# A linear-attention and maxout kernel that runs from a written table: another table, buffer lists cut to their users, and the gate copies taken out

## Chip, core and metric

One core of one Trainium2 chip. The metric is the device time of one execution, in microseconds; of three executions of the kernel before, the median is 287.12.

## What is computed

Two parts, one behind the other. Attention with a feature map, per batch `b` and head `h` (8 by 8, 576 tokens, 64 columns), and then a maxout layer over the 4608 tokens with all heads side by side (512 columns, 768 hidden):

```python
def phi(x):                       # w_phi: 64 x 128
    proj = x @ w_phi
    proj = proj - max(abs(proj), axis=-1)
    return concat(exp(proj), exp(-proj))
kv  = phi(k).T @ v                # 256 x 64 per head
num = phi(q) @ kv
den = phi(q) @ sum(phi(k), over tokens) + 1e-6
x   = (num / den), heads side by side      # 4608 x 512
h   = maximum(maximum(x @ w1, x @ w2), x @ w3)
out = h @ w_out
```

Inputs and output are float32; the matmuls run in bfloat16.

## The kernel before

The attention is cut into 16 units of four heads (`u` = 0 to 15; two units make a batch). The names below are those of the steps, as `Node` has them in its first argument:

- `L`, `L0`, `Lv`: loads of q, k and v. Unit 0 loads q and k in two halves each, in float32, through SP, and casts them (`C`, on DVE or ACT). Units 1 to 3 load q and k through POOL with a cast on the way, straight into `qk_bf`. From unit 4 on the loads are float32 and POOL casts. v is always loaded in float32 (`v_raw`), through SP or, in early units, POOL.
- `T`, `Tc`: the transposes. For units 0 to 3 PE transposes into PSUM and DVE copies to `qkT`; later units use the DMA transpose from SP (line 508).
- `G`: projections by `w_phi`, into `psq` and `psk`; `r`: DVE's absolute maxima (line 554) into `mqp` and `mk`; `ek`: ACT's exponentials of k (line 548).
- For q: in units 0 and 1 the maximum is subtracted by small products (lines 616 and 619); from unit 2 on PE turns the maxima (`R`), a copy makes `mT`, a small DMA (`V`, line 570, from SP or ACT) stores them as a row of `qkT`, and `M` (line 614) projects with them. `eq` is ACT's exponential of `M`.
- `E`, `va`, `vd`: ACT's correction factors `em`, POOL's multiplication of v by them (line 589).
- `K`, `kv`, `N`, `x`, `X`: the sums over tokens, their copy, the numerators with the denominator as a column, the division, and the transpose of the result into `xT` (PE in units 0 and 1, the DMA transpose at line 691 later).

The maxout layer is cut into nine chunks of 512 tokens (eight batches' first 512, and the rest of all). It uses differences of weights (`wd`, POOL or DVE, line 785): `up`/`up2` are the products by w2-w1 and w3-w1 (line 714), with the maxima on DVE and ACT, and `down` sums the straight product of x by w1 w_out (line 742) and the hidden part by w_out (line 747). w1 w_out is made on the chip (`wt`, `we`, `wm`, `mo`). `W` are the weight loads on POOL, in number four.

No loop sets the order. `PLAN` is a written table with one word for each of the 1473 steps: `163T4@18.3` is step 163 on PE (T; D is DVE, A is ACT, G is POOL, S is SP), the first buffer of its list that has no slot yet gets slot 4, and 18.3 us is the moment for which the table laid it out. `plan` reads the words in order and gives each step its engine and slots; the steps are then emitted in that order, so that each engine's queue is fixed. The moment is not enforced on the chip: an engine takes its next step as soon as what the step needs is there and its buffers are free. It is used once more, in `fill`, which puts idle products (line 842, a 128x512 matmul of ones into a PSUM bank that is free) into gaps of PE's queue that are over 0.35 us in the table (over 0.5 from 28 us on), one each 0.43 us up to 4.6 us and one each 0.26 us later.

The list `bufs` of a step says which buffers it uses; in this kernel it is read only by `plan`, to hand out the slots in the word, and by `fill`, for PSUM. A tile is made at its first use when the steps are emitted.

Three gates hold loads back. For u = 1, 2 and 3 a DVE copy of one element from `qkT` of unit u - 1 into `v_raw` of unit u is placed ahead of that unit's v load, which has to wait for it:

```python
gates.append(nd("gate", {"DVE": 0.1}, lambda src=src, col=col, raw=raw: nc.vector.tensor_copy(
    raw()[0:1, 0, 0:1], src()[0:1, col:col + 1]), [], [src, raw]))
```

Of the kernel before, what the change touches and what calls it, by code (L numbers as in the profile page):

```python
# [105 lines left out]
138A@23.2 103D@23.4 139T3@23.7 49A@23.7 105A@23.8 160G@23.9 130T4@23.9 162D@24.0 141A@24.3 127T5@24.3 140A@24.5  # L106
228D3@24.7 108D@24.8 131A@24.8 69T007@24.9 229S@24.9 119A1@25.3 111A@25.6 120G1@25.7 137A@26.0 133T3@26.3 71D@26.4
129A@26.5 113D@26.7 121G@26.8 182T006200@26.8 70A@27.0 74T70@27.1 134A@27.2 185D@27.3 1095T0@27.4 123A@27.7 186D@27.9
135A@28.0 124G@28.1 132A@28.5 75D0@28.5 76T6@28.7 184A@29.0 78T3@29.1 125G@29.2 72T4@29.4 1096A@29.4 79D1@29.6
1093T7@29.7 126A@29.9 110A@30.0 77D0@30.2 122G@30.3 1077G@30.5 183A@30.5 73D1@30.8 128A@31.0 177T03@31.1 1081G@31.2  # L110
172T16@31.3 179A@31.5 142T124@31.6 175D@31.7 174A@32.0 181D@32.3 1094A@32.5 176D@32.9 1079G@33.3 167T51@33.4 180D@33.5
144A@33.6 187T7@33.7 178A@33.8 80T4@34.0 190D@34.1 82T0@34.3 168A@34.3 81D@34.5 1097T3@34.5 83A@34.8 170D@34.8
143A@35.3 363G0@35.4 191D@35.4 171D@35.8 151T41@35.8 1098A@36.0 147T0@36.2 152D0@36.4 149T5@36.5 189A@36.5 364G@36.5
192T2@36.8 173A@36.8 145T3@36.8 148D1@37.0 1091T4@37.2 169A@37.3 150D0@37.6 1080G@37.6 188A@37.7 193D0@38.2 146D1@38.4
194S@38.5 230T6@38.5 1092A@38.7 232T0@39.1 195A0@39.1 231D0@39.3 365S1@39.3 234T1@39.6 197G0@39.7 155T7@39.8 233D@39.9
# [758 lines left out]
```

## Time and profile before

| | |
|---|---|
| three executions | 286.9, 287.12 and 290.07 us, median 287.12 |
| profiled execution, first to last instruction | 285.3 us (its own device time is not listed; the median lies 1.8 us above this span) |
| PE busy | 274.8 us, 96% |
| DVE, ACT, POOL busy | 208.4, 192.5, 125.0 us |
| idle products | 28, 9.51 us busy |
| mean granted clock of PE | 0.992 |
| DMA | 51.46 MB, 180 GB/s on average |
| last matmul's end to the end of the span | 3.4 us |

PE is nearly always busy. Matmuls are pipelined, so a busy PE is not PE at its peak, and the idle products are in its busy time as well. In rows of the timeline, `start, length, engine line op out<-in xcount [idle before <-releaser]`; PEld is PE's weight load, SPq and ACTq are issues of DMAs.

### The profile page before, as it was taken

The numbers are of one execution on the slowest core, as the hardware profiler recorded it, in microseconds if no ns is written. First come the engines' busy times: TensorE is split into PE (matmuls) and PEld (weight loads), VectorE is DVE, ScalarE is ACT, GpSimd is POOL, SyncE is SP. The second block draws the span as 40 slices with busy tenths as digits, with TensorE's granted clock in tenths as the row PEclk, the third lists the DMA queues.
The fourth block names the chain that finished last, engine by engine and source line by source line (L and its number), as shares of the span: only waits on it lengthen the run. The fifth ranks groups of instructions, "written<-read, shape, count | busy, mean of one in ns | idle before, by whom it ended". The sixth has DMA issues, their size and how long they took to land.

```text
span 285.3 us, 8441 instructions
## 1 busy us (share of the span) xinstructions
PE 274.8 (96%) x3485; PEld 155.7 (55%) x3522; DVE 208.4 (73%) x442; ACT 192.5 (67%) x445; POOL 125.0 (44%) x107
## 2 busy tenths in 40 slices
PE   8889999999999999999999999999999999999995
PEld 3557674565565555456565565555544664444442
DVE  2897899988999868688678779987975472227431
ACT  3798979997999987878868887779775400041001
POOL 9338999945923574417534950160080501000000
PEclk9997999999999999999999999999999999999999
DMA  7999979999899998988897998294420134153135
GB/s 192 203 284 262 312 144 305 341 239 250 221 293 196 225 232 280 251 156 202 258 251 272 268 199 182 99 182 81 82 62 3 27 54 90 37 110 76 37 85 173
DMA packets 67760, 51.46 MB, mean 180 GB/s; under 512 B 48778, under 2 KB 53002, under 8 KB 67722
## 3 DMA queue, kind: packets, MB, share of 16 engines
q1 hardware_dynamic: 62734, 43.38, 60.6%
q0 software_dynamic: 4576, 7.28, 12.1%
q8 instruction: 27, 0.44, 0.6%
q10 hardware_dynamic: 412, 0.28, 0.3%
q14 instruction: 11, 0.09, 0.1%
HBM read 34.67 MB, written 9.44 MB: 155 GB/s over the span
## 4 chain that ended last, share of the span: by engine, by line
PE 81%; DMA 8%; ACT 6%; POOL 1%; DVE 1%; issue 1%; ACTq 0%; POOLq 0%
PE ups L714 29%; PE ops L747 15%; PE ops L742 10%; PE psn L661 6%; PE kvps L643 6%; DMA qk_bf<-in_q_dram 5%; PE psm L614 5%; PE psq L535 4%; DMA qkT<-mT 3%; ACT Eq L627 3%; PE pm L811 2%; ACT Ek L548 2%; PE tps L493 1%; PE psq L530 1%; POOL qk_bf L458 1%
## 5 line engine op out<-in xcount | busy, mean ns | idle before, releaser
L714 PE MATMUL ups<-xT,w_bf 128*128 128x512 bf16 x415 | 101.5, 379 | 1.4 <-ACT Ek L548 0.5
L627 ACT ACTIVATE Eq<-psm 128x512 bf16<-128x512 f32 (+1 forms) x160 | 81.9, 582 | 15.6 <-PE psm L614 12.8
L589 POOL TENSOR_TENSOR vab<-v_raw,em 128x1152 bf16<-128x1152 f32 (+1 forms) x36 | 68.1, 1907 | 36.8 <-ACT em L585 27.9
L548 ACT ACTIVATE Ek<-psk 128x512 bf16<-128x512 f32 x128 | 73.5, 622 | 8.5 <-PE psk L535 5.8
L714 PEld LDWEIGHTS <-w_bf 128*128 128x128 bf16 x432 | 40.6, 98 | 45.4 <-issue 1.0
L720 DVE TENSOR_TENSOR hT<-hT,ups 128x512 bf16<-128x512 bf16 x54 | 36.4, 683 | 24.6 <-ACT hT L722 13.6
L554 DVE TENSOR_REDUCE mqp<-psq 128x4 bf16<-128x512 f32 (+1 forms) x80 | 49.0, 633 | 5.1 <-PE psk L535 2.9
L747 PE MATMUL ops<-wout_bf,hT 128*128 128x512 bf16 (+2 forms) x215 | 51.5, 373 | 0.5 <-issue 0.2
L554 DVE TENSOR_REDUCE mk<-psk 128x4 f32<-128x512 f32 x64 | 43.0, 683 | 0.7 <-PE psk L535 0.5
L747 PEld LDWEIGHTS <-hT 128*128 128x128 bf16 x222 | 21.1, 98 | 23.1
L668 DVE TENSOR_TENSOR x_sb<-psn,rden 128x320 bf16<-128x320 f32 x64 | 31.5, 492 | 2.2
L722 ACT ACTIVATE hT<-ups 128x512 bf16<-128x512 f32 x31 | 18.5, 615 | 21.1 <-PE ups L714 21.0
L755 ACT COPY osb<-ops 128x512 f32<-128x512 f32 (+2 forms) x17 | 9.6, 581 | 30.2 <-PE ops L747 12.7
L661 PEld LDWEIGHTS <-Eq 128*128 128x128 bf16 x640 | 24.9, 97 | 8.0
L755 DVE COPY osb<-ops 128x512 f32<-128x512 f32 x20 | 13.6, 689 | 20.1 <-PE ops L747 18.5
L661 PE MATMUL psn<-kv_sb,Eq 128*128 128x65 bf16 x640 | 26.8, 194 | 0.1
L742 PE MATMUL ops<-xT 128*128 128x512 bf16 x88 | 24.2, 379 | 0.4
L614 PE MATMUL psm<-qkT,wphi_m 128*128 128x512 bf16 (+1 forms) x70 | 22.3, 359 | 0.7 <-DMA qkT<-mT 0.6
L535 PE MATMUL psq<-w,qkT 64*128 64x128 bf16 x256 | 21.5, 217 | 0.5 <-DVE qkT L496 0.2
L476 POOL CAST qk_bf<-q_raw 128x1152 bf16<-128x1152 f32 x12 | 13.8, 1148 | 18.1 <-DMA q_raw<-in_q_dram 9.7
L535 PE MATMUL psk<-w,qkT 64*128 64x128 bf16 x256 | 21.3, 217 | 0.4 <-DVE mqp L554 0.4
L535 PEld LDWEIGHTS <-qkT 64*128 64x128 bf16 x512 | 14.8, 94 | 10.7 <-issue 8.1
(76 smaller groups left out, 272.6 us busy)
## 6 DMA issues: line engine op xcount, KB each, us to landing
out_dram<-osb SPq DMA_DIRECT2D x64, 128.0 KB, 2.5
v_raw<-in_v_dram SPq DMA_DIRECT2D x14, 576.0 KB
k_raw<-in_k_dram SPq DMA_DIRECT2D x11, 576.0 KB, 4.9
q_raw<-in_q_dram SPq DMA_DIRECT2D x11, 576.0 KB, 4.9
w_bf<-in_moe_w_dram POOLq DMA_DIRECT2D x3, 768.0 KB, 11.1
v_raw<-in_v_dram POOLq DMA_DIRECT2D x2, 576.0 KB, 13.7
qk_bf<-in_k_dram POOLq DMA_DIRECT2D x3, 288.0 KB, 13.4
qk_bf<-in_q_dram POOLq DMA_DIRECT2D x3, 288.0 KB, 13.6
```

Of the source, the lines that this page charges most:

```text
L535: nc.tensor.matmul(ps()[:, i, :], lhsT=cols[r, :], rhs=w2[r, c, :], start=True, stop=True)
L548: nc.scalar.activation(Ek[s]()[:, tiles_of(t0, n), :], of(1), EXP, scale=1.0 - 2.0 * s)
L554: nc.vector.tensor_reduce((mq, mk)[c]()[:, tiles_of(t0, n)], of(c), AXX, ALU.max, apply_absolute_value=True)
L589: (nc.vector if n_.eng == "DVE" else nc.gpsimd).tensor_tensor(vab()[:, g, t0:t1, 0:D], vb()[:, t0:t1, :], em()[:, g, t0:t1].unsqueeze(2).t ...
L614: nc.tensor.matmul(psm()[:, 0:w], lhsT=wphi_m, rhs=rhs, start=True, stop=True)
L627: nc.scalar.activation(Eqb()[s][:, cols], psm()[:, 0:w], EXP, scale=1.0 - 2.0 * s)
L661: nc.tensor.matmul(psn()[:, c, :], lhsT=Eqb()[g][:, t0:t0 + P], rhs=kv()[:, pr, ab, g, :], start=(g == 0), stop=(g == 1))
L668: nc.vector.tensor_tensor(x_sb()[:, pr, :, ab, :], psn()[:, :, 0:D], rden().to_broadcast([P, 5, D]), ALU.mult)
L714: nc.tensor.matmul(ups(), lhsT=w_bf[i + 1][:, ct, j * P:(j + 1) * P], rhs=tokens_of(ct), start=(ct == 0), stop=(ct == CT - 1))
L720: nc.vector.tensor_tensor(hT()[:, j, :], hT()[:, j, :], ups(), ALU.max)
L742: nc.tensor.matmul(ops_()[:, 0:width], lhsT=tile_of(ct, tt), rhs=line_w[c_i > MOVE][:, ct, cols], start=(ct == 0), stop=False)
L747: nc.tensor.matmul(ops_()[:, 0:width], lhsT=hT()[:, j, tt * P:(tt + 1) * P], rhs=wout_bf[:, j, cols], start=False, stop=(j == JT - 1))
```

## The change

The table has other words throughout: another order, other engines for some steps and other slots. The gates and their constant are gone, so there are 1470 steps, and numbers above the gates' shift by one to three. Buffers are taken out of the lists of steps that do not themselves touch them: `mk`, `mqp` and `Ek` from `G`, `Eq` from `M`, `kv_sb` from `K`, and `x_sb` from `N`. What each step computes, its dependences otherwise, the idle products' rule and the costs are as before.

```diff
-GATES = (None, (0, 0), (1, 0), (2, 0))
 PLAN = """
-0G@0.7 4A@0.7 6S0@0.7 2D0@0.8 3D@1.0 10S0@1.2 1G@1.3 12S@1.6 85G0@1.9 8S@2.1 84G@2.6 1075G@3.3 158G1@4.0 5D@4.1
-157G@4.7 7A2@5.0 14G0@5.5 1078G@6.2 11A@6.3 1076G@6.9 15T1@7.2 13A@7.3 361G1@7.7 16D0@7.8 360G1@8.4 21T002300@8.6
-26T45@8.8 24D@9.0 9A@9.1 29D@9.6 28A@9.7 19T6@10.0 17T7@10.2 27A@10.2 20D@10.4 22A@10.7 227G2@10.7 41T1@10.7 18D@10.8
-23A@11.1 226G@11.4 30D@11.4 31T24@11.5 36T67@11.8 32A@12.0 34D@12.0 90T5@12.1 33A@12.4 39D@12.6 88T2@12.7 38A@12.9
-44D@13.2 37A@13.4 89D1@13.5 54T60@13.9 43A@13.9 40D@14.1 92T2@14.4 55A@14.5 86D1@14.7 93D@14.8 63T7@14.9 87S@14.9
-25D@15.0 56A@15.0 114T11211@15.3 42A@15.5 35D@15.6 60T6@15.6 64A@15.7 1085T3@16.1 91D@16.2 65A@16.2 99T40@16.6
-62A@16.7 45D@16.8 57T7@17.0 117D@17.1 61A@17.2 1089T5@17.4 159D2@17.4 102D@17.5 59A@17.6 104T16@17.9 1090D0@18.1
-58A@18.1 163T4@18.3 46A0@18.6 118D@18.7 94T75@18.8 50A@18.9 164D2@19.0 115A@19.2 53G0@19.3 47G@19.5 116A@19.5
-1086D@19.6 95A@19.7 165T4@19.8 66T2@20.0 96A@20.2 107D@20.2 48G@20.6 67A@20.7 166D@20.8 68A@21.0 109T31@21.0 97D@21.0
-100A@21.2 1087T4@21.3 112D@21.6 51G@21.7 101A@21.7 106A@22.2 1088D@22.2 136T21@22.6 52G@22.8 98D@22.8 161T7@23.1
...
-1445T6@264.1 1411D0@264.3 1418T@265.0 1412S@265.0 1446D@265.2 1405T7@266.3 1419A1@266.5 1420S@267.1 1406T@267.2
-1462T@268.5 1457T1@269.7 1458T@270.6 1413T3@271.9 1459D3@272.1 1407D2@272.7 1414T@272.8 1460S@272.8 1463D0@273.3
-1408S@273.4 1453T2@274.1 1415D1@274.3 1464S@274.6 1454T@274.9 1416S@275.2 1469T5@276.2 1455D3@276.4 1470T@276.4
-1465T6@276.8 1471A2@277.0 1456S@277.1 1466T@277.4 1472S@277.7 1467A0@278.6 1468A@279.0
+0G@0.7 2D0@0.7 4A@0.7 8S0@0.7 3D@0.8 12S0@1.1 1G@1.3 10S@1.6 6S@2.0 14S0@2.5 9D0@3.2 84G1@3.2 5D@3.8 85G@3.9 13D@4.3
+1072G@4.6 17T1@4.8 11D@5.0 156G2@5.4 18D0@5.5 157G@6.1 31T23@6.2 7A@6.5 36T45@6.5 34D0@6.7 86G1@6.9 37A0@7.0 15T6@7.2
+35D0@7.3 1075G@7.6 19T7@7.8 16D@7.9 32A@8.0 1073G@8.4 38A0@8.5 39D@8.5 21T12@8.7 20D@9.1 23A@9.1 357G1@9.2 24D@9.3
+41T6@9.5 22A@9.6 26T47@9.8 44D@9.9 33A@10.1 29D@10.2 43A@10.5 87T1@10.6 28A@10.8 40D@10.8 54T3@11.2 27A@11.3 88D1@11.4
+57T4@11.7 42A@11.8 55A0@12.0 25D@12.0 98T51@12.2 56A@12.5 45D@12.6 60T2@12.8 30D@12.9 59A@13.0 89T6@13.3 50A0@13.4
+102D1@13.5 46A@13.7 91T3@13.8 58A@13.9 48G0@14.0 101D1@14.1 63T7@14.2 61A@14.3 1086T4@14.6 90D@14.7 64A@14.8 1082T5@15.1
+47G@15.1 100A1@15.3 92D@15.3 1087D0@15.5 93T63@15.7 65A@15.8 66T0@16.1 1083D@16.1 49G@16.2 62A@16.3 1084T4@16.4 51G@16.4
+67A@16.7 96D@16.7 113T7@16.9 99A1@17.0 108T52@17.2 1085D@17.3 68A@17.5 53G@17.5 52G@17.6 103T61@17.7 115A@17.7 111D@17.9
+159T0@18.0 95A@18.0 114A@18.5 161T4@18.5 106D@18.5 94A@18.7 224G0@18.8 163T5@19.0 116D@19.1 109A@19.2 164D2@19.5
+225G@19.5 138T6@19.6 117D@19.7 110A@19.7 132T5@19.9 97D@20.0 140A1@20.2 158G2@20.2 129T7@20.4 139A@20.4 162D@20.6
+118A1@20.7 69T36@20.9 130A@21.0 120G1@21.1 160D@21.2 131A@21.5 112D@21.8 104A@22.0 180T40@22.0 358G1@22.2 126T7@22.4
+70D0@22.4 71D@22.7 135T2@22.8 119G@22.9 128A@23.0 107D@23.1 76T3@23.2 1092T6@23.6 183D0@23.7 122A@23.8 181A0@24.0
...
+1447D@259.7 1454T3@260.2 1416A1@260.4 1417S@261.0 1410T0@261.1 1407T@261.9 1411T@263.2 1408A2@263.4 1409S@264.0
+1403T@264.5 1458T1@265.8 1404D3@266.0 1412A0@266.0 1455T@266.7 1405S@266.7 1413S@267.9 1466T2@268.0 1456D1@268.2
+1450T5@268.2 1459T@269.0 1457S@269.1 1451T@270.3 1460A2@270.5 1461S@271.2 1462T6@271.6 1452A3@271.8 1467T@272.3
+1453S@272.5 1463T@272.6 1468D0@272.8 1469S@273.3 1464A1@273.8 1465S@274.2
...
 
         qk = buf("qk_bf", QK, [P, 2, UT, D] if by_pe and u else [P, UT, 2 * D], BF16)
         qkT = un["qkT"] = buf("qkT", 3, [P, UT * P], BF16)
-        mains, cast, gates = [], {}, []
+        mains, cast = [], {}
         for what in range(3):
             raw = raw_bufs(u)[what]
             if what < 2 and by_pe:
@@ -461,12 +456,7 @@
                                                        packet=PACKET_BF)
                 mains.append(None)
             else:
-                if by_pe and u < len(GATES) and GATES[u]:
-
-                    src, col = units[GATES[u][0]]["qkT"], BATCHES[GATES[u][1]][0] * P
-                    gates.append(nd("gate", {"DVE": 0.1}, lambda src=src, col=col, raw=raw: nc.vector.tensor_copy(
-                        raw()[0:1, 0, 0:1], src()[0:1, col:col + 1]), [], [src, raw]))
-                n_ = nd("Lv" if what == 2 else "L", {"SP": 0.62, "POOL": 0.75} if what < 2 and u <= AHEAD or u < 3 else {"SP": 0.62}, None, gates, [raw],
+                n_ = nd("Lv" if what == 2 else "L", {"SP": 0.62, "POOL": 0.75} if what < 2 and u <= AHEAD or u < 3 else {"SP": 0.62}, None, [], [raw],
                         pipe=(EARLY if u == 0 or u == BY_PE and what == 1 else 1.0) * FULL, hold=-3.0, lat=1.7,
                         packet=PACKET)
                 n_.fn = lambda n_=n_, what=what, raw=raw: queue_of[n_.eng].dma_start(by_pairs(raw()), rows_of(what, u, 0, 2))
@@ -500,9 +490,6 @@
                 c_ = nd("Tc", {"DVE": 0.62 if nb == 8 else 0.22}, None, [a], [tps, qkT], locks=[tps])
                 c_.fn = lambda n_=c_, f=tc_: f(n_)
                 tr[i] = c_
-            un["Tc"] = tr
-            for g in gates:
-                g.deps.append(units[GATES[u][0]]["Tc"][GATES[u][1]])
         else:
             def tdma():
                 nc.sync.dma_start_transpose(out=qkT().rearrange("p (t c) -> p t c", c=P),
@@ -537,7 +524,7 @@
             tiles = [ps for x in given for ps in x[2:] if ps]
             ti = 2 if n == 2 else t0 // NT
             a = nd("G", {"PE": 0.22 if n == 2 else 0.236 * len(part)}, lambda mms=mms: [f() for f in mms], [tr[ti], n_phi],
-                   [qkT, mk, mq] + tiles + Ek, mode=int(n == 4))
+                   [qkT] + tiles, mode=int(n == 4))
             projs.append(a)
             un.setdefault("G", []).append(a)
             for t0, n, psq, psk in given:
@@ -619,9 +606,9 @@
                     nc.tensor.matmul(psm()[:, i * wide:(i + 1) * wide], lhsT=mq()[:, t:t + 1].to_broadcast([P, P]),
                                      rhs=minus[:, ch], start=False, stop=(t == of[-1]))
             if by_product:
-                a = nd("M", {"PE": 0.12 * n}, mm, reds[0::2] + [n_phi, n_minus], [qkT, psm, Eqb, mq])
+                a = nd("M", {"PE": 0.12 * n}, mm, reds[0::2] + [n_phi, n_minus], [qkT, psm, mq])
             else:
-                a = nd("M", {"PE": 0.22 if n == 4 else 0.12}, mm, [n_v, n_phi], [qkT, psm, Eqb])
+                a = nd("M", {"PE": 0.22 if n == 4 else 0.12}, mm, [n_v, n_phi], [qkT, psm])
             for s in range(2):
                 def eq(s=s, cols=cols, w=w, psm=psm):
                     nc.scalar.activation(Eqb()[s][:, cols], psm()[:, 0:w], EXP, scale=1.0 - 2.0 * s)
@@ -642,7 +629,7 @@
                         r = slice(ab * D, (ab + 1) * D)
                         nc.tensor.matmul(kvps[ab]()[:, t // NT, g, :], lhsT=Ek[g]()[r, t, :], rhs=vab()[r, g, t, :],
                                          start=(t + g == 0), stop=(t == UT - 1 and g == 1))
-        n_k = nd("K", {"PE": KPE}, kmm, exps + n_va, [vab, kv] + kvps + Ek, mode=1)
+        n_k = nd("K", {"PE": KPE}, kmm, exps + n_va, [vab] + kvps + Ek, mode=1)
         for ab in range(2):
             def kv_out(n_, ab=ab):
                 copy_on[n_.eng](kv()[:, :, ab].rearrange("p r g d -> p r (g d)"), kvps[ab]().rearrange("p r g d -> p r (g d)"))
@@ -668,7 +655,7 @@
                     nc.vector.tensor_tensor(x_sb()[:, pr, :, ab, :], psn()[:, :, 0:D], rden().to_broadcast([P, 5, D]),
                                             ALU.mult)
                 first_eq = 4 * pr + 2 * ab
-                a = nd("N", {"PE": 0.32}, nmm, [n_kvs[ab]] + eqs[first_eq:first_eq + 2] + eqs[8:], [Eqb, kv, psn, x_sb])
+                a = nd("N", {"PE": 0.32}, nmm, [n_kvs[ab]] + eqs[first_eq:first_eq + 2] + eqs[8:], [Eqb, kv, psn])
                 divs[pr].append(nd("x", {"DVE": 0.62}, div, [a], [psn, x_sb, rden], locks=[psn]))
 
         done = []
```

In the new table the first words of each queue are these. SP: unit 0's second halves (8, 12), then its first halves (10, 6), then its v (14). POOL: unit 1's q and k (84, 85), w1 (1072), unit 2 (156, 157), unit 1's v (86), w_out (1075), w2 (1073), one load of unit 5 (357), then the v products of unit 0. DVE casts three of unit 0's halves (9, 13, 11), with w_phi's cast (5) behind the first, and ACT one (7); before, ACT cast all four. Before, unit 0's v stood on POOL (14G0@5.5) and unit 1's on SP behind its gate. The rule of `fill`, read over the words, gives 17 idle products where it gave 28.

Further down, two kinds of words come up in the prediction. One is the pair of mT's store (`V`) and the first `M` of a unit, old and new:

| unit | old words | lead | new words | lead |
|---|---|---|---|---|
| 7 | 523A@110.2, 540T@112.6 | 2.4 | 520A@105.2, 537T@108.4 | 3.2 |
| 8 | 588S@96.3, 599T@100.8 | 4.5 | 585S@93.6, 590T@96.0 | 2.4 |
| 11 | 783A@169.4, 800T@173.8 | 4.4 | 780A@166.3, 794T@168.8 | 2.5 |
| 12 | 848S@179.7, 865T@183.6 | 3.9 | 845S@180.9, 862T@183.2 | 2.3 |
| 13 | 913S@151.1, 927T@155.6 | 4.5 | 910S@147.2, 924T@149.5 | 2.3 |
| 15 | 1043A@210.8, 1057T@214.2 | 3.4 | 1040S@205.3, 1054T@207.8 | 2.5 |

The other is unit 8's DMA transpose and its first `G`: 560S@73.7 and 581T@81.5 before, 557S@73.7 and 578T@78.6 now, with the loads 488S@68.9, 424S@69.3 and 554S@69.9 ahead of it on SP.

More of the change, by code (lines that the diff above doesn't have):

```diff
@@ L106 @@
[L106 to L115, printed above, removed]
@@ new lines @@
+876S@197.5 1030A@197.9 1022D@198.0 1422G@198.0 1314T4@198.3 979G@198.3 1026D@198.6 975S@198.9 1316T6@199.2 1313D@199.2
+1315D@199.8 1033T1@200.0 1322T0@200.2 1317D@200.4 1027D@201.0 1318T2@201.1 1310T4@202.0 1319D@202.2 1036D@202.8
+1340T6@202.8 1032D@203.1 1311D@203.7 1348T2@203.7 1341A1@203.9 1035A@204.4 980T5@204.6 1349D@204.8 1038T4@204.8
+1346T6@204.8 1039A1@205.0 982A0@205.2 1040S@205.3 1034A@205.6 1342T4@205.7 1347D@205.9 1327T@206.6 1343D@206.8
+1037D@207.4 1041A1@207.8 1054T2@207.8 1328A3@208.0 1048T6@208.1 1043G1@208.2 1045T4@208.3 1323T@208.5 1024A@208.5
@@ new lines @@
+1378T7@237.8 1442T5@238.6 1379D@238.8 1381D@239.4 1384T6@239.5 1430T7@240.3 1385A@240.5 1376A1@241.0 1444T0@241.2
+1377S@241.6 1414T6@242.1 1367T@242.9 1382T3@244.2 1429A1@244.4 1431D@244.4 1437D@245.0 1396T1@245.1 1368D1@245.6
+1432T7@246.0 1383D@246.2 1369S@246.4 1388T2@246.8 1443D@246.8 1433A@247.0 1397D@247.4 1373S@247.6 1390T4@247.7
+1400T3@248.5 1391D@248.7 1365S@248.8 1445D@249.3 1434T5@249.4 1389D@249.9 1325S@250.0 1448T7@250.3 1435A@250.5
+1401D@250.7 1392T1@251.1 1449D@251.3 1394T4@252.0 1440T0@252.9 1395D@253.1 1426T2@253.7 1446T5@254.6 1427A@254.8
```

240 lines of the change are left out of this document (117 added, 123 removed).

## The prediction

> **What bounds the kernel now.** I read the page first, then the merged chain in order of time, then the timeline of the first 30 us, then windows over that stretch, then the tail.
>
> ```profile
> span 285.3 us, 8441 instructions
> PE 274.8 (96%) x3485; PEld 155.7 (55%) x3522; DVE 208.4 (73%) x442; ACT 192.5 (67%) x445; POOL 125.0 (44%) x107
> 0.00:285.30 285.30, 9.51 (x28) 0.99 0.74 180
> 30.00:62.00 32.00, 31.70 (x548) 19.89 (x553) 30.59 (x67) 29.78 (x71) 29.76 (x21) 1.00 0.99 258
> 110.00:118.00 8.00, 7.13 (x69) 3.62 (x63) 6.20 (x13) 5.96 (x18) 6.55 (x5) 1.00 0.89 247
> 118.00:260.00 142.00, 140.79 (x1664) 77.64 (x1684) 99.52 (x209) 88.62 (x200) 44.92 (x37) 1.00 0.59 142
> ```
>
> The third row is the idle products alone (28, 9.51 us); the window rows give, behind the bounds and the length, the busy time of PE, PEld, DVE, ACT and POOL, the granted clock, the DMA share and GB/s. PE is 10.5 us short of the span. From 30 us on almost nothing is missing: 0.30 in 30 to 62, 0.87 in 110 to 118, 1.21 in 118 to 260. A reordering can take little there. What can go stands in the first 30 us (idle time and most of the 9.51 us of idle products), beside a tail of 3.4 us behind the last matmul.
>
> ```profile
> 5.00 13.59 DMA qk_bf<-in_q_dram
> 18.64 0.66 PE tps L493 x16
> 22.61 0.43 PE idler L842
> 59.92 5.33 DMA qkT<-mT
> 280.73 1.14 PE L747 MATMUL ops<-wout_bf,hT 128*128 128x384 bf16 x6
> 281.95 0.48 ACT L755 COPY osb<-ops 128x384 f32<-128x384 f32 x1 [1.40 <-PE ops L747]
> ```
>
> The first four rows are the chain, the last two the tail. The chain starts on unit 2's q load, issued by POOL at 5.00 and landed at 18.6; then PE takes over and keeps it apart from a few waits, the longest of them 5.33 for one mT store. So the start is set by when the loads queued on POOL are done, and everything after it is shifted with that moment.
>
> **The first stage, row by row.**
>
> ```profile
> 1.04 5.52 PE L842 MATMUL idler<-idle 128*128 128x512 bf16 x17 [1.04 <-DVE idle L412]
> 1.90 0.94 POOL L458 DMA_DIRECT2D qk_bf<-in_k_dram  x1
> 3.53 0.67 ACT L451 CAST qk_bf<-q_raw 128x576 bf16<-128x576 f32 x1 [0.24 <-DMA q_raw<-in_q_dram]
> 4.64 0.67 ACT L451 CAST qk_bf<-k_raw 128x576 bf16<-128x576 f32 x1 [0.44 <-DMA k_raw<-in_k_dram]
> 5.71 0.76 POOL L472 DMA_DIRECT2D v_raw<-in_v_dram  x1
> 6.11 0.41 DVE L405 CAST w<-wphi_f 64x128 bf16<-64x128 f32 x1 [2.14 <-DMA wphi_f<-in_w_phi_dram]
> 7.14 0.69 DVE L496 COPY qkT<-tps 128x1024 bf16<-128x1024 bf16 x1 [0.39 <-PE tps L490]
> 7.64 0.67 ACT L451 CAST qk_bf<-k_raw 128x576 bf16<-128x576 f32 x1 [2.33 <-DMA k_raw<-in_k_dram]
> 9.29 0.67 ACT L451 CAST qk_bf<-q_raw 128x576 bf16<-128x576 f32 x1 [0.98 <-DMA q_raw<-in_q_dram]
> 11.47 0.45 PEld L535 LDWEIGHTS <-qkT 64*128 64x128 bf16 x16 [0.62 <-DVE qkT L496]
> 14.66 0.13 DVE L467 CAST v_raw<-qkT 1x1 f32<-1x1 bf16 x1
> 15.91 0.61 PE L797 MATMUL pwT<-ident,w_bf 128*128 128x128 bf16 x8
> 17.37 0.13 DVE L467 CAST v_raw<-qkT 1x1 f32<-1x1 bf16 x1
> 18.64 0.64 PE L493 MATMUL tps<-ident,qk_bf 128*64 128x128 bf16 x16 [0.46 <-DMA qk_bf<-in_q_dram]
> 20.06 0.30 PE L493 MATMUL tps<-ident,qk_bf 128*64 128x128 bf16 x4 [0.46 <-DVE qkT L496]
> 25.65 0.14 DVE L467 CAST v_raw<-qkT 1x1 f32<-1x1 bf16 x1
> ```
>
> The four half loads of unit 0 land at 3.53, 4.64, 7.64 and 9.29; w_phi's second half only at 6.11. The three tiny DVE casts into v_raw are the gates. Their table entries, 86D1@14.7, 159D2@17.4 and 228D3@24.7, let me set the table's clock against the chip's: 14.66, 17.37, 25.65. So the table is a usable map; where it says 278.6 for the last evacuation (1467A0) the chip has 281.95, 3.3 later. I use it as a map of what stands ahead of what, and take no time from it for the sum.
>
> **The change part by part.** Helpers, counts and shapes of the real work stay. The buffer lists only decide which slot digits a table word needs, so by themselves they emit nothing. What changes is order, engine and slot.
>
> *The gates go.* Three DVE casts of 0.13 leave (0.4 us on DVE, hidden while PE is the bound, and a gain of that size where DVE is), and with them the hold on v. Unit 0's v moves from POOL's sixth load to SP's fifth (14S0@2.5) and unit 1's v takes the old place on POOL (86G1). POOL's words 84 and 85 stand at 3.2 and 3.9, but no dependence holds them there: POOL will issue them at about 1.9, as in the row above. So unit 0's halves see the same neighbours in the same queue positions as before, and I expect third and fourth half again at about 7.6 and 9.3, where the table casts them at 5.0 and 6.5.
>
> *v's place in the traffic.* It now runs ahead of unit 1, w1 and unit 2.
>
> ```profile
> 4.47:7.88 3.41, 3.28 (x21) 1.43 (x19) 1.32 (x3) 0.91 (x2) 3.41 (x5) 1.00 1.01 201
> 18.12:21.54 3.42, 2.12 (x43) 1.49 (x39) 3.13 (x7) 3.28 (x12) 1.97 (x3) 1.00 1.14 287
> 21.54:24.95 3.41, 3.41 (x39) 2.57 (x36) 2.98 (x6) 2.34 (x6) 3.41 (x5) 0.50 1.19 211
> 28.36:31.80 3.44, 3.39 (x53) 2.25 (x51) 2.87 (x9) 3.44 (x11) 3.29 (x5) 1.00 1.07 341
> ```
>
> The DMA share is 1.0 or more in each of these, so a load put ahead delays what is behind it. 576 KB at the fastest rate shown (341 GB/s) is 1.7 us, at 201 it is 2.9. Unit 2's q then lands at 20.3 to 21.5 instead of 18.6. Unit 0's v itself comes sooner, but no row has PE waiting for it. The Trainium skill (DMA: Bandwidth & Descriptors, "Issuing engines are not separate DMA queues") says that DMAs started from several engines run on the same 16 DMA engines and interleave, which speaks against a gain from putting v on SP; by the opposite reading unit 2 would land at 18.6 still.
>
> *DVE takes three of unit 0's casts from ACT*, in the order 9D, 5D (w_phi), 13D, 11D, 18D. The queue is in order: 13D stands behind w_phi (6.11 and 0.41, then a cast more), 11D waits for the third half at 7.64, and 18D, the first qkT copy, stands behind 11D. No DVE cast of 128x576 is in the trace; the nearest rows are the ACT cast of that shape (0.67) and the DVE copy of 128x1024 (0.69), below it the 64x128 cast (0.41). I take 0.6. The first copy then starts at 8.2, 1.1 us after the 7.14 of before, although the new table has it 2.3 earlier (5.5 for 7.8). From 7.64 DVE has, ahead of the last G of unit 1 in PE's queue (103T, whose bank is freed by 96D): the cast, 4 copies of 0.69, 2 of 0.28, 11 long reductions at 0.645, 2 short at 0.42, 2 turned copies at 0.68, in all 13.2 us, so 20.9. Unit 2's transposes follow at about 21.2. These durations come from the rows here:
>
> ```profile
> 8.32 1.29 DVE L554 TENSOR_REDUCE mqp<-psq 128x4 bf16<-128x512 f32 x2 [0.49 <-PE psq L535]
> 10.29 0.29 DVE L496 COPY qkT<-tps 128x256 bf16<-128x256 bf16 x1 [0.68 <-PE tps L490]
> 17.04 0.41 DVE L554 TENSOR_REDUCE mqp<-psq 128x2 bf16<-128x256 f32 x1
> 19.92 0.68 DVE L800 COPY hT<-pwT 128x1024 bf16<-128x1024 bf16 x1
> 112.22 1.54 ACTq L570 DMA_DIRECT2D qkT<-mT  x1
> PE psm L614 <- DMA qkT<-mT: 0.6, 2, 0.3
> 115.77 0.70 PE L614 MATMUL psm<-qkT,wphi_m 128*128 128x256 bf16 x3 [0.29 <-DMA qkT<-mT]
> 61.30 5.50 SPq L508 DMA_TRANSPOSE qkT<-qk_bf  x1
> ```
>
> **The sum**, against PE's last matmul at 281.87 and the span of 285.3 (the three runs give 286.9 to 290.07, median 287.12, 1.8 us more than this span; I carry that 1.8 along).
> - Unit 2's first transpose from 18.64 to 20.8, between the landing (20.3) and DVE (21.2): +2.2. Bounds 19.3 and 23: +0.7 to +4.4.
> - Work that now stands ahead of it: a turn of w1 (0.61, some 0.55 in a stream), two G's (0.45 for 16 loads, two G's) and a short M (0.3): -1.3.
> - Idle products behind it: three before (one at half clock 0.43, row at 22.61; two at full clock, so 0.22 each), none in the new table, which has 17 in all, nine of them ahead of the first transpose: -0.9.
> - PE's idle time behind it: the window from 18.12 lacks 1.30, of which 0.46 is the landing; of the 0.84 left (0.46 of it for DVE at 20.06) I let two thirds go, since DVE stays full: -0.6 (0 to -0.85).
> - The half-clock window, 21.54 to 24.95 at 0.50: between the second and third gate the chip took 8.28 us for 7.3 of the table, 0.46 of it the wait for unit 2, so 0.5 to 1.0. It will likely fall earlier, where DVE and loads bind: -0.75 (+1.5 to -1.0).
> - Waits for transfers later: the table's lead from mT's store to the first M is now 2.3, 2.3, 2.4, 2.5 and 2.5 us in five units (3.0 to 3.2 in four more), where it was 2.4 once and 3.4 or more otherwise. That one time M ran 3.55 us after the issue (115.77 less 112.22), with an issue of 1.54; an issue half as long gives 2.8. At 2.8 the five cost 2.0, less 0.4 of before; partly absorbed: +1.0 (0 to +5).
>
> Total -0.35: **286.8 us**. The tail keeps its order: -0 there. Below one another the ends give 283 to 291.
>
> **Rivals.**
> 1. *The table's early start holds* (0.22): the halves land as the words have them, DVE is not late, and all moves with unit 2 and the idle products as the last words do (1467A0@278.6 to 1464A1@273.8), -4.8: 282.3. It would have to come out of the idle products (9.51) and PE's idle time ahead of 30 us. For it: the gates' agreement within 0.05 us up to 17.4. Against: 7.64 and 9.29 in the rows, for 5.0 and 6.5.
> 2. *Slower: PE's head waits for returns of transfers* (0.20). Place: M behind mT's store, and G behind the DMA transpose, whose shortest lead falls from 7.8 us (unit 8, 73.7 to 81.5) to 4.9 (73.7 to 78.6), now with three loads ahead on SP from 68.9 on; the row at 61.30 shows an issue of 5.50 behind such loads. Price: five M at 3.55 less their leads are 5.75, less 1.15 of before, 4.6; in place of the +1.0 that is 290.4. It decides from about 3 us of mT latency on. Against: PE's waits for mT sum to 0.6 in before.
> 3. *More half-rate clock* (0.10). PE's nine first idle products end at about 4.9 (1.04 and nine of 0.43), real work comes at about 7.3, and waits go on to 14; before it was 3.28 of 3.41 busy in that window. If two windows of the busy stretch after 12 us run at 0.50, each costs up to 1.0 as above: 288.8. The Trainium skill (TensorE: Matmul & The Clock Gate, Part 1) has the clock halved after an idle window of about 3.4 us and freed after a busy one; the trace agrees in the one case it has, 0.50 in a window of 3.41 us behind one with 2.12 busy.
>
> **How the numbers follow.** The forecast itself has 0.48. Two per cent of 287.12 is 5.7 us, about what a measurement of this kernel can tell from no change. Faster by that means under 281.4, less than even rival 1 gives: 0.07. Slower means over 292.9, the far end of rival 2 with rival 3: 0.08. Within: 0.85. The range takes in rivals 1 and 2 at their prices: 282.2 to 290.6.
>
> **What would show it.** Right: third and fourth half landing at 7.6 and 9.3, the first qkT copy on DVE at about 8.2 behind a cast that waited, unit 0's v landed by 11, unit 2's first transpose at 20 to 22, half clock before 18 us rather than at 21.5, 17 idle products of which some 4 us in the first five, more PE waits for mT than 0.6. Wrong: a first copy before 6.5 and unit 2 before 19 (rival 1), or over 3 us of PE waiting for transfers behind 40 us (rival 2).

## The result, and the profile after

| | median | runs | ratio to before (95%) |
|---|---|---|---|
| before | 287.32 us | 286.9 to 290.07 | |
| after | 299.64 us | 297.97 to 302.85 | 1.040 [1.034, 1.046] |

The row of before has one run more than the three above. The new table is slower by 12.3 us, outside the range of the prediction (282.2 to 290.6) and beyond rival 2's 290.4. The profiled execution took 299.32 us, with a span of 297.5. Medians and ranges take in all runs, while the ratios leave out slow ones, those over 1.5% above the fastest of their kernel; the profiled run of the trial with idle products ahead of unit 5's M is a slow one.

The head of the page, and the line on the chain that ended last:

```profile
span 297.5 us, 8452 instructions
PE 277.7 (93%) x3511; PEld 156.0 (52%) x3511; DVE 207.0 (70%) x437; ACT 191.8 (64%) x442; POOL 126.2 (42%) x112
...
PE 66%; DMA 16%; ACT 9%; DVE 3%; POOL 3%; issue 2%; SPq 0%; POOLq 0%; DVEq 0%; ACTq 0%
```

PE is busy for 2.9 us more and idle for 9.3 us more (297.5 less 277.7, against 285.3 less 274.8). This split is rough, since the trace of before lacks some 37 matmul records (3485 beside 3522 weight loads). Before, the chain was 81% PE and 8% DMA; now DMA has 16% of it and ACT 9%. So the loss is to be looked for in waits for transfers.

**Where it lies.** I cut both executions at the first up-product and at PE's last matmul. Windows over that stretch, before first, then after (bounds, length, busy time of PE, PEld, DVE, ACT, POOL, clock, DMA share, GB/s):

```profile
42.86:281.87 239.01, 235.91 (x2835) 129.97 (x2867) 174.98 (x361) 158.67 (x367) 93.39 (x71) 1.00 0.70 172
```
```profile
42.70:294.16 251.46, 240.71 (x2874) 131.71 (x2871) 172.46 (x356) 161.01 (x370) 94.58 (x75) 0.99 0.69 167
```

The first up-product starts at 42.70 where it started at 42.86: nothing is won or lost up to there. Behind it the same work takes 251.46 us for 239.01. All of the +12.4 lies there, in the part to which the sum gave +1.0. (Most of the missing records lie in the first row, so of the two rows only the lengths are compared.)

The waits of PE in the after-kernel (what was waited for: us in total, times, longest), then the transfers in the chain behind 60 us, in order of time (start, us):

```profile
PE psm L601 <- DMA qkT<-mT: 5.0, 4, 1.9
PE psq L517 <- DMA qkT<-qk_bf: 2.9, 2, 2.5
PE tps L480 <- DVE qk_bf L446: 2.7, 1, 2.7
PE psn L648 <- issue: 1.3, 1, 1.3
...
PE kvps L630 <- POOL vab L586: 1.0, 1, 1.0
```
```profile
63.18 6.66 DMA qkT<-mT
...
84.69 7.44 DMA qkT<-qk_bf
...
96.37 4.57 DMA qkT<-mT
...
130.15 7.45 DMA v_raw<-in_v_dram
...
164.52 2.68 DMA qkT<-mT
...
173.37 6.22 DMA qkT<-qk_bf
...
184.56 4.50 DMA qkT<-mT
```

M waits 5.0 us for mT's store, for 0.6 before; G waits 2.9 for DMA transposes, mostly for unit 8's (2.5). The stores that PE waits for are those of units 5, 6, 13 and 11. One of them takes 2.68 us, the others 4.5 to 6.7. (The wait of 2.7 lies in the start. The load of v at 130.15 stands ahead of the va product for which K waits 1.0.)

**Unit 5 shows the pattern.** From the timeline (start, us), rows of SP's queue, of ACT's and of PE in the after-kernel, then the same place before:

```profile
59.46 0.57 SPq L462 DMA_DIRECT2D q_raw<-in_q_dram  x1
...
61.31 0.55 SPq L462 DMA_DIRECT2D v_raw<-in_v_dram  x1
61.97 7.63 SPq L495 DMA_TRANSPOSE qkT<-qk_bf  x1
...
63.18 1.34 ACTq L557 DMA_DIRECT2D qkT<-mT  x1
...
68.13 0.36 PE L648 MATMUL psn<-kv_sb,Eq 128*128 128x65 bf16 x6 [1.30 <-issue]
69.88 0.38 PE L601 MATMUL psm<-qkT,wphi_m 128*128 128x512 bf16 x1 [1.39 <-DMA qkT<-mT]
```
```profile
59.92 0.77 SPq L570 DMA_DIRECT2D qkT<-mT  x1
...
65.30 0.39 PE L614 MATMUL psm<-qkT,wphi_m 128*128 128x512 bf16 x1 [0.35 <-DMA qkT<-mT]
```

Before, the store was issued by SP ahead of unit 6's DMA transpose (T6), 5.38 us ahead of M, and PE missed it by 0.35. Now ACT issues it behind the transpose and four loads of 576 KB, it takes 6.70, and PE stands at M for 1.39 with everything behind it. In this unit the lead on the chip did not shrink: M's turn came 5.31 us after the store's issue, 1.30 of them the wait by "issue" at 68.13, against 5.03 before; the store took longer. In units 6, 11 and 13 M's turn came 3.19, 2.68 and 2.41 us after the issue. The wait in unit 5 then costs a second time; the two rows below the windows are from the chain:

```profile
66.85:70.27 3.42, 0.75 (x8) 0.46 (x9) 2.08 (x6) 0.35 (x1) 3.42 (x3) 1.00 1.20 232
70.27:73.69 3.42, 3.42 (x19) 1.73 (x18) 1.27 (x5) 2.98 (x6) 1.51 (x3) 0.51 1.30 145
```
```profile
70.25 1.51 PE ops L729 x4
...
105.34 0.86 PE ops L729 x4
```

In the window with the waits PE was busy for 0.75 of 3.42 us, and in the next its clock was 0.51. Four products of one kind take 1.51 us in that window and 0.86 at full clock. By this ratio some 1.5 of the 3.42 us (an estimate) are lost after the wait is over. Rival 3 had this mechanism, but at the start. Added up, 5.0 for mT, 2.9 for transposes, 1.3 for issue, 1.0 for va and 1.5 of half clock are 11.7, of which before had 0.6.

### The profile page after: what moved, and what is told of

Same layout as the page of the kernel before. It is cut to its first block, busy times and chain, and to the rows that moved or that the text cites. A ratio compares the mean times of both kernels' runs of the same rounds, so it can differ in the third digit from the quotient of the medians.

```text
span 297.5 us, 8452 instructions
## 1 busy us (share of the span) xinstructions
PE 277.7 (93%) x3511; PEld 156.0 (52%) x3511; DVE 207.0 (70%) x437; ACT 191.8 (64%) x442; POOL 126.2 (42%) x112
## 4 chain that ended last, share of the span: by engine, by line
PE 66%; DMA 16%; ACT 9%; DVE 3%; POOL 3%; issue 2%; SPq 0%; POOLq 0%; DVEq 0%; ACTq 0%
PE ups L701 24%; PE ops L734 13%; PE ops L729 8%; DMA qkT<-mT 6%; DMA qkT<-qk_bf 5%; PE psn L648 4%; PE kvps L630 4%; ACT Eq L614 4%; ACT Ek L535 4%; PE psm L601 4%; PE psq L522 3%; DMA v_raw<-in_v_dram 3%; DMA k_raw<-in_k_dram 2%; POOL vab L576 2%; PE pm L798 2%
## 5 line engine op out<-in xcount | busy, mean ns | idle before, releaser
L614 ACT ACTIVATE Eq<-psm 128x512 bf16<-128x512 f32 (+1 forms) x160 | 83.4, 605 | 13.6 <-PE psm L601 12.7
L535 ACT ACTIVATE Ek<-psk 128x512 bf16<-128x512 f32 x128 | 73.7, 629 | 7.4 <-PE psk L522 3.5
L707 DVE TENSOR_TENSOR hT<-hT,ups 128x512 bf16<-128x512 bf16 x54 | 35.3, 682 | 9.6 <-PE ups L701 9.3
L709 ACT ACTIVATE hT<-ups 128x512 bf16<-128x512 f32 x26 | 16.0, 619 | 31.9 <-PE ups L701 28.0
L742 ACT COPY osb<-ops 128x512 f32<-128x512 f32 (+1 forms) x26 | 15.8, 608 | 30.6 <-PE ops L734 25.4
L711 DVE TENSOR_SCALAR hT<-ups 128x512 bf16<-128x512 f32 x28 | 19.0, 686 | 23.4 <-PE ups L701 19.1
L648 PEld LDWEIGHTS <-Eq 128*128 128x128 bf16 x640 | 26.3, 98 | 10.4 <-issue 2.0
L648 PE MATMUL psn<-kv_sb,Eq 128*128 128x65 bf16 x640 | 28.0, 194 | 1.3 <-issue 1.3
L729 PE MATMUL ops<-xT 128*128 128x512 bf16 x96 | 25.1, 387 | 0.0
L654 DVE RECIPROCAL rden<-psn 128x5 f32<-128x5 f32 x64 | 12.0, 188 | 14.5 <-PE psn L648 14.2
L630 PE MATMUL kvps<-vab,Ek 64*128 64x65 bf16 x1152 | 20.4, 190 | 1.3 <-POOL vab L586 1.0
```

What stands on the lines that cost most here:

```text
L535: nc.scalar.activation(Ek[s]()[:, tiles_of(t0, n), :], of(1), EXP, scale=1.0 - 2.0 * s)
L614: nc.scalar.activation(Eqb()[s][:, cols], psm()[:, 0:w], EXP, scale=1.0 - 2.0 * s)
L630: nc.tensor.matmul(kvps[ab]()[:, t // NT, g, :], lhsT=Ek[g]()[r, t, :], rhs=vab()[r, g, t, :], start=(t + g == 0), stop=(t == UT - 1 and g ...
L648: nc.tensor.matmul(psn()[:, c, :], lhsT=Eqb()[g][:, t0:t0 + P], rhs=kv()[:, pr, ab, g, :], start=(g == 0), stop=(g == 1))
L707: nc.vector.tensor_tensor(hT()[:, j, :], hT()[:, j, :], ups(), ALU.max)
L729: nc.tensor.matmul(ops_()[:, 0:width], lhsT=tile_of(ct, tt), rhs=line_w[c_i > MOVE][:, ct, cols], start=(ct == 0), stop=False)
```

## The experiments

Theory A, formed on this trace: PE's queue is in order, M and G stand too few steps behind the transfers that feed them, and each wait is multiplied. Rivals: the stores cost by themselves (issue time, packets); the start; POOL's or SP's queue; the clock.

**Are the stores the cause? (new table, old table)** In both, `n_v.fn` does nothing, so row 64 of qkT keeps older data and M waits for no transfer.

```diff
-            n_v.fn = lambda: queue_of[n_v.eng].dma_start(
-                qkT()[D:D + 1, :].rearrange("o (t c) -> o t c", c=P), mT())
+            n_v.fn = lambda: None
```

> The new table with the 14 small DMAs that store mT into qkT left out (units 2 to 15 then leave out the subtraction of the row maximum for q), so that M waits for nothing but G. Theory A (PE's head waits for mT and for the DMA transposes are most of the loss behind 43 us): the idle time for mT (1.39, 1.42, 0.31, 1.87 us, 5.0 in all by the waits) goes, and the half-clock window at 70.3 to 73.7 that follows the longest of them; 5 to 8 us faster than the new table, 291.5 to 294.5 us; G's waits for the DMA transposes stay at 2.9 us or grow. Theory B (the waits are only where some other lateness shows, each wait would come back at the next step): under 2 us, 298 or more.

> The old table with the same 14 stores left out: the control. Theory A: old leads are long, 0.6 us of waits for mT in the profile and 5.33 us of one store on the chain, so 0.5 to 1.5 us faster than before, about 286. Theory B (the stores cost by themselves, as traffic or on SP and ACT): as much as in the new table, 3 us or more.

Measured: the new table 288.93 us, ratio 1.009 [1.006, 1.012], so 10.7 less than with stores; the old 285.6, ratio 0.994 [0.991, 0.997], 1.6 less. Both won more than foretold. In the traces the late part, from the first up-product to PE's last matmul, takes 242.00 and 237.38 us, 9.5 and 1.6 less than with stores. Stores and waits for them cost the new table 9 us more than the old by the medians and 7.8 by the late parts: some two thirds to three quarters of the loss. What remains between the two, 3.3 us by the medians, has another cause and is taken up under "Open".

**The wait, or the store itself?** The store goes into a tile that nobody reads.

```diff
+    aside = const.tile([UT, P], BF16, name="aside")
 ...
-                qkT()[D:D + 1, :].rearrange("o (t c) -> o t c", c=P), mT())
+                aside, mT())
```

> The new table, each mT store still issued where it is, by the same engine and with the same 18 packets of 256 bytes, but into a tile of its own that nobody reads (so m is left out of the query side, and M waits for no transfer). Theory A, the wait alone costs: like the kernel without the stores, 288 to 290.5 us, first M after the store's issue without a wait. Theory B, the stores cost by ACT's and SP's time for issuing them (0.75 to 1.5 us each, 14 of them) and by their packets: 296 to 300, and PE's gaps go to other waits for ACT and DVE.

Measured: 293.13 us, 1.0235 [1.0145, 1.0325]. Between the two theories: some 6.5 us are the waits, some 4 the issue and the packets of the stores, though with this interval (2.6 us to either side) the second share is poorly known. PE's late part was 244.55 us in the trace, 6.9 shorter than with the wait, and of PE's waits those for transposes, unit 8's first, remained:

```profile
PE psq L518 <- DMA qkT<-qk_bf: 2.9, 2, 2.1
```

**Can order alone mend it?** For the first of two lists, PE, ACT and DVE were listed again behind 39 us, with a step allowed to pass others where its input would be late by a store of 4.5 us. No diff is shown, since 77 words of PE, 107 of DVE and 204 of ACT stand elsewhere.

> The new table up to 39 us word for word; behind it the same steps on the same engines, in the same slots, with the order of PE, ACT and DVE (not of POOL and SP) listed again for an mT store that takes 4.5 us from issue to M: a step that would have to wait lets up to three others pass on PE, eight on ACT, two on DVE. Nothing is left out. Theory A, M's lead behind the store is too short for the chip: PE's waits for mT fall from 5.0 us to under 1.5, the end comes 6 to 9 us earlier, 290.5 to 293.5. Theory B, what was lost comes back at other places (ACT and DVE late, banks): PE's gaps stay above 14 us in sum and the time at 297 to 300.

Measured: 296.05 us, 1.033 [1.026, 1.040]. PE's waits for mT fell from 5.0 to 1.7 us, near what was expected, but only 3.6 us came back. PE's waits in that kernel:

```profile
PE psq L521 <- DMA qkT<-qk_bf: 2.0, 2, 1.4
PE psm L605 <- DMA qkT<-mT: 1.7, 2, 1.0
PE ops L733 <- ACT Eq L618: 1.4, 1, 1.4
...
PE psk L526 <- DVE mqp L545: 0.4, 1, 0.4
```

Waits for ACT and DVE have come in where those for mT were. The second list goes one step further:

> As the relisted table (4.5 us for a store, order of PE, ACT and DVE listed again behind 39 us), with up to four steps passed on PE, and unit 8's second cast ahead of va on POOL as in the run where it was moved alone. Theory A, what is left in the relisted table are waits that an order can still take away (1.39 for T8, 1.04 and 0.63 for mT): these three fall under 1 us in sum and the time to 293.5 to 295.5. Theory B, each wait taken away turns up at another engine's step: the sum of PE's gaps stays at 12 to 14 us and the time at 295.5 to 297.

Measured: 296.5 us, 1.035 [1.030, 1.040]. mT waits are down to 0.8 us, the one for unit 8's transpose (T8) stands at 1.83, and the time is the same: theory B. PE's waits:

```profile
PE psq L521 <- DMA qkT<-qk_bf: 2.2, 2, 1.8
...
PE psm L605 <- DMA qkT<-mT: 0.8, 2, 0.5
```

Passing other steps takes the waits for mT away, but brings only 3.6 and 3.1 us of the 12.3. In the traces the late part is 249.81 and 249.91 us, only some 1.6 shorter than after's; the rest lies in the start, whose words are the same. That the passed steps of ACT and DVE are late next fits the waits listed, but was not shown step by step. Neither list beats the old table.

**Does a short lead cost in the old table too?** Five M moved forward on PE by two or three steps, nothing else (PE's words around unit 13's M, as an example; 1249 and 1250 are a down-product):

```diff
-726T3 1249T0 1250T 927T40
+726T3 927T40 1249T0 1250T
```

> The old table with the first M of units 6, 8, 13, 11 and 12 moved forward on PE by one to three steps, so that the words' leads behind the mT store are 3.4, 3.3, 2.3, 2.7 and 3.1 us, for 4.1, 4.5, 4.5, 4.4 and 3.9 (nearly those of the new table); nothing else is touched. Theory A, the lead is what PE waits for, in any table: PE's waits for mT rise from 0.6 to 2 to 4 us, and the time by 1.5 to 4 us, to 288.8 to 291.3. Theory B, the waits come from the rest of the new order (ACT late, loads beside the store): mT waits stay under 1 us and the time within 0.7 us of before.

Measured: 289.85 us, 1.012 [1.007, 1.018], 3.1 more than its runs of before. The waits for mT rose only to 1.3 us (PE's waits):

```profile
PE psm L615 <- DMA qkT<-mT: 1.3, 3, 0.8
...
PE psm L615 <- DVE mk L555: 0.6, 1, 0.6
...
PE psm L615 <- DVE mqp L555: 0.5, 1, 0.5
```

The time came as theory A had it, the waits for mT below its 2 to 4. In the trace the late part is 3.0 us longer (241.97 for 239.01). The waits for mT make 0.7 of this, and 1.4 are waits of M for DVE (the two rows above) and for ACT (0.3), none of which stands in the list of before: an M that is placed earlier stands there before other inputs as well. So order alone makes waits in the old table too. That a wait for mT by itself costs more than its length is not shown by this.

**What stretches a store?** Four loads more, ahead of unit 15's store, where the DMA engines stood still.

```diff
 ...
+                if u == UNITS - 1:
+                    for n_u, what in ((u - 1, 0), (u - 1, 1), (u, 0), (u, 1)):
+                        nc.sync.dma_start(by_pairs(raw_bufs(n_u)[what]()), rows_of(what, n_u, 0, 2))
 ...
```

> The new table with four loads more (q and k of units 14 and 15 once again, 576 KB each, into buffers that are through) issued by SP directly ahead of unit 15's mT store, where the DMA engines stood still (0.00 from 221 to 227 us) and M ran 2.54 us after the store's issue. SP reaches them some 5 us before the store. Theory A, full DMA engines stretch the store: M of unit 15 comes 4.5 to 6.7 us after the store's issue, as beside the loads of units 5 and 6, PE waits 2 to 4 us for it, and the end is later by as much. Theory B, the store's time is its own whatever else runs: M stays within 3.2 us, and PE's end is as before within its own scatter of some 1.5 us.

Windows ahead of the store and the timeline rows of the store and its M, of the after-kernel first, then with the loads:

```profile
223.00:225.00 2.00, 2.00 (x11) 0.94 (x10) 1.73 (x4) 0.76 (x2) 0.00 (x0) 1.00 0.00 0
225.00:227.00 2.00, 2.00 (x12) 0.93 (x11) 1.38 (x2) 1.13 (x4) 0.00 (x0) 1.00 0.00 0
```
```profile
228.20 0.81 PE L601 MATMUL psm<-qkT,wphi_m 128*128 128x512 bf16 x3
```
```profile
223.00:225.00 2.00, 2.00 (x12) 0.94 (x11) 1.18 (x3) 1.74 (x5) 0.00 (x0) 1.00 1.02 392
225.00:227.00 2.00, 2.00 (x10) 0.76 (x8) 1.67 (x3) 0.17 (x2) 0.00 (x0) 1.00 0.91 354
```
```profile
224.37 0.80 SPq L561 DMA_DIRECT2D qkT<-mT  x1
...
228.31 0.82 PE L610 MATMUL psm<-qkT,wphi_m 128*128 128x512 bf16 x3 [1.23 <-DMA qkT<-mT]
```

In the after-kernel M ran 2.54 us after its store (issued at 225.66) without a wait. With the engines at 0.91 to 1.02 it ran after 3.94 and PE waited 1.23. So loads stretch the store by at least 1.4, and PE waits less than the 2 to 4 that I expected. Unit 5's 6.70 is 4.2 above the quiet 2.54, so loads explain about a third of that; T6 was under way there as well. What the transpose adds was not measured by itself, nor what it adds that ACT and not SP issues the stores of units 5 and 6 now. The reverse trial, without the four loads ahead of unit 5's store, gave no time. In after's own trace the stores go by the load: the DMA share between issue and M was 0.01, 0.21 and 0.67 for units 15, 13 and 12 (2.54, 2.72 and 2.34 us), and 1.03, 1.11 and 1.10 for units 11, 6 and 5 (4.55, 4.61 and 6.70). The median with the loads, 301.43 us (1.053 [1.046, 1.060]), is 1.8 above after.

**Is T8 late because its cast is late?** Its second cast stood on POOL behind va, for which POOL waited 7.61 us for ACT.

```diff
-327G1 328G 556G
+556G 327G1 328G
```

> The new table with one word moved: unit 8's second cast (556G) stands on POOL ahead of unit 4's two va products, for which POOL waited 7.6 us for ACT's em, instead of behind them. Theory A, T8's transfer is late because its cast stands in POOL's queue behind va, which waits for a late ACT: the transpose is issued at about 82.3 us (behind the loads on SP) instead of 84.69, PE's wait for T8 of 2.52 us falls under 0.6, and the time by about 2 us, to 297 to 298. Theory B, SP's queue or the transfers themselves set it: the wait stays over 2 us and the time at 299 to 300.

The transpose in SP's queue, after-kernel first, then with the cast moved, and PE's wait there:

```profile
84.69 3.84 SPq L495 DMA_TRANSPOSE qkT<-qk_bf  x1
```
```profile
81.53 6.31 SPq L495 DMA_TRANSPOSE qkT<-qk_bf  x1
```
```profile
PE psq L517 <- DMA qkT<-qk_bf: 2.4, 2, 2.0
```

It was issued 3.2 us earlier, right behind the loads (expected 82.3), and then took 6.31 us for 3.84: its issue ended at 87.8 for 88.5, where the loads ahead of it stood 0.45 earlier in this run anyway. PE still waited 2.0, and the median is 300.73 (1.046 [1.033, 1.058]). This is theory B: something in SP's queue or in the transfers sets it, not the cast. To put the transpose ahead of those loads was not tried.

**The start: gates, casts, clock.** Old table without gates (`gate` does nothing), new table with three casts back on ACT, new table with twelve idle products more ahead of the first transpose:

```diff
-                    gates.append(nd("gate", {"DVE": 0.1}, lambda src=src, ...: nc.vector.tensor_copy(...
+                    gates.append(nd("gate", {"DVE": 0.1}, lambda: None, [], [src, raw]))
```
```diff
-9D0 13D 11D
+9A0 13A 11A
```
```diff
+    todo += [(4.6 + 0.01 * k, make(6)) for k in range(12)]
```

> The old table with nothing else changed but the three gate copies left out, so that unit 1's v (SP) is issued at about 2.8 us and units 2 and 3's v whenever their buffer and queue allow. Theory A: v runs ahead of unit 2, whose q load then lands 1 to 2 us later than 18.6; the start of the chain moves with it: 1 to 2 us slower, 288 to 289.5. Theory B (traffic ahead is harmless, since PE, DVE and ACT bind there too): within 0.5 us.

> The new table with three of unit 0's casts (words 9, 13 and 11) back on ACT, in their places. Theory A, the start is late because DVE's casts stand in order ahead of its first copy: first qkT copy at 7.2 to 7.8 us instead of 8.96, unit 2's first transpose at 21.3 to 22.2 instead of 22.86, and the first up-product 0.6 to 1.5 us before 42.76; the time 298 to 299. Theory B, loads and DVE's later work set the start: unit 2's first transpose within 0.4 us of 22.86 and the time unchanged (299 to 300).

> The new table with 12 idle products more, put behind the nine that stand ahead of the first transpose, so that PE works from 1.0 to about 7.7 us. Theory A (two half-clock windows from 8.9 to 15.7 us are part of what the start lost): granted clock 1.0 there, unit 2's first transpose at 21 to 22 in place of 22.9, 0.7 to 1.8 us faster than the new table. Theory B (loads and DVE bind there, the clock is hidden): within 0.5 us.

The gates were worth 2.8 us: 290.06, 1.010 [1.006, 1.013]. Unit 2's transposes went from 18.64 to 20.82 and the first up-product from 42.86 to 44.87. With the casts on ACT the first copy came at 6.67 for 8.96 and unit 2 at 21.91 for 22.86, but the median is 299.24 (1.044 [1.035, 1.052]), no different. The idle products held the clock at 1.0, yet unit 2 came at 22.71 and the first up-product at 43.12, so what half clock costs at the start is no more than the scatter there: from the first copy to unit 2's transposes after took 13.90 us at a clock of 0.76, and two other runs with its words 13.85 and 13.95 at 1.00. That kernel's four runs lie between 296.97 and 305.23 (median 302.22), too far apart for more. In eight runs that share the new words of the start, unit 2's transposes began between 20.78 and 22.86, so one run's start says little within 2 us; their first up-product lies between 40.93 and 42.70, that of the three runs with the old start between 41.66 and 42.86.

**Does filling the wait keep the clock?** Six idle products ahead of unit 5's first M.

```diff
+    todo += [(60.55, make(3)) for k in range(6)]
```

> The new table with six idle products (0.22 us each at full clock) put into PE's queue right ahead of unit 5's first M, where PE stood still in the window 66.85 to 70.27 with 0.75 us busy, and ran at half clock in the next. Theory A, the waits cost twice, once as idle time and once as the half-clock window behind them: with some 2 us busy in that window the clock stays at 1.0 after 20 us, and 1.3 to 1.7 us come back, 297.9 to 298.4. Theory B, the clock behind the wait costs nothing that PE would not wait for later anyway: the window is gone or not, and the time stays at 299 to 300.5.

Two windows of that kernel, then PE's timeline there:

```profile
66.17:69.59 3.42, 1.45 (x14) 0.52 (x11) 2.26 (x6) 0.53 (x2) 3.42 (x3) 1.00 1.19 212
69.59:73.00 3.41, 3.19 (x8) 0.86 (x7) 0.00 (x0) 0.78 (x2) 1.69 (x3) 0.50 1.36 179
```
```profile
68.38 3.16 PE L830 MATMUL idler<-idle 128*128 128x512 bf16 x6
71.60 0.58 PE L602 MATMUL psm<-qkT,wphi_m 128*128 128x512 bf16 x1
```

300.52 us, 1.045 [1.037, 1.054]: nothing won, and the trial does not answer its question. In its profiled execution the wait ended by "issue" (1.85) came ahead of the idle products, the window held 1.45 us of work, the clock fell all the same, and the six products then took 3.16 us at half clock and themselves held M back.

## Why the prediction was wrong, step by step

- **Gates, casts and unit 2: within the bounds, for one of two reasons.** I had unit 2's first transpose at 20.8 (19.3 to 23); it was 22.86. A first copy at 8.2 behind a cast that waited for the third half was 8.96; the cast of 128x576 on DVE took 0.75 for 0.6, and that half landed at 8.3 for 7.6. Unit 2's q was there at 18.0, not at 20.3, so the landing, which I had made one end of the estimate, was wrong. What held unit 2 was work: from the first copy to 22.86 DVE was busy for 12.29 and PE for 13.02 of 13.90 us, and no row tells which of them set the time. In the old table without gates the landing does set it (20.82, where PE waits for q), so my 20.8 fits that kernel better than this one. The timeline rows of DVE and PE:

```profile
6.96 0.73 DVE L446 CAST qk_bf<-k_raw 128x576 bf16<-128x576 f32 x1
...
7.75 0.62 PE L480 MATMUL tps<-ident,qk_bf 128*128 128x128 bf16 x8 [2.69 <-DVE qk_bf L446]
...
8.29 0.75 DVE L446 CAST qk_bf<-k_raw 128x576 bf16<-128x576 f32 x1 [0.60 <-DMA k_raw<-in_k_dram]
8.96 0.68 DVE L486 COPY qkT<-tps 128x1024 bf16<-128x1024 bf16 x1
```

- **The start as a sum.** The first five terms gave -1.35; the first up-product moved by -0.16 in the profiled runs, less than the scatter of this start. The 17 idle products were as foretold. Rival 1 (-4.8) is refuted. One sum was added wrongly: the high ends of the six terms make +8.7, or 295.8, and not 291; the result lies beyond that too.
- **Half clock earlier, and cheap: right.** It fell into the two windows from 8.88 to 15.71 instead of 21.5, and with it held off the first up-product came no earlier (43.12). The windows:
```profile
5.47:8.88 3.41, 1.13 (x11) 0.66 (x11) 1.69 (x4) 0.00 (x0) 2.59 (x4) 1.00 1.00 254
8.88:12.30 3.42, 2.74 (x29) 2.01 (x28) 2.19 (x5) 1.91 (x4) 0.71 (x1) 0.50 1.16 246
```

- **The step that failed: "Waits for transfers later", +1.0 (0 to +5).** The mechanism, M's lead behind its store, was right, and the size was not: PE's waits for stores and transposes rose by 7.3 us (5.0 and 2.9, for 0.6), and the stretch in which they lie by 12.4. Two things were mis-sized in the term, and one had no term.
  - *The price of a store.* I took 2.8 us for every store, from one row (3.55, less part of its issue). For the five units that I priced (8, 11, 12, 13 and 15) the sum was nearly right, by luck: 2.0 expected, 1.87 (unit 11) and 0.31 (unit 13) measured, none in the other three. But units 5 and 6, with leads of 3.4 and 3.0, passed as safe, and they cost 1.39 and 1.42. The 2.8 holds at a low DMA share (2.34 to 2.72 us) and not at one over 1 (4.55 to 6.70). The row that contradicted it stood in my second fence: the store at 59.92 had taken 5.33 in just that stretch of full DMA engines. I quoted it as the longest wait and did not use it as a price; 5.33 against a lead of 3.4 is 1.9.
  - *Transposes* (2.9 us) were left to rival 2, whose chain, M behind the store and G behind the transpose, is what happened. Its price for the five M, 5.75, is near the 5.0 measured, though for partly other units, which is luck; it put nothing on the transposes and on what follows a wait.
  - *What comes with the waits* had no term. Of the 5.1 us beyond the 7.3 the trace names 1.3 by "issue", 1.0 for va and 1.5 of half clock; 1.3 stay unnamed. Whether a wait costs more than its length is open: 5.0 us of waits taken away with the store aside brought 6.5, give or take 2.6, and the two lists, which took away 3.3 and 4.2 us of waits for mT, brought 3.6 and 3.1.
- **The chances.** Rival 2 had 0.20, and its sign, over 3 us of PE waiting for transfers behind 40 us, came with 7.9. Against it stood that PE's waits for mT sum to 0.6 before. That row said that the old leads were long enough; it did not say how long a store takes.
- **Open.** The 1.30 us at 66.8 that ended by "issue" stand in all runs with the new order at that place (0.8 to 1.9), at 0.6 in one of the two relisted tables and in none of the old; I have no cause for them. The 3.3 us that the new table loses without any store are only partly named: the wait of 1.4 for unit 8's transpose and 1.1 of "issue" in that run.

## What to carry to other kernels

Before an order is judged, take for each kind of transfer the longest time from issue to a consumer that waited for it that the old trace shows, in stretches as loaded as the one in question, not the typical one, and hold it against the new lead of every consumer (a consumer that did not wait gives only an upper bound); a consumer at the head of an in-order queue is safe only above the longest. "No wait" in the old profile is a statement about the old leads, not about the transfer. And look at what a wait on the bounding engine brings with it: here one was followed by a window at half clock, and lists that took waits away brought other waits in.
